# Attention and a 2-D Fourier filter on one core: stack rows loaded in pieces of 16 and 12, four butterflies and three transposes moved

## The chip, the cores and the metric

The kernel runs on one core of a Trainium2 chip, as one program. The metric is the device time of one execution in microseconds (us). The kernel before has a median of 712.09 us over three runs.

## The reference

Two results are computed and put side by side.

- Part A: attention with a compressive memory. `x` has 2048 rows of 576 numbers. `q`, `k` and `v` are `x` times three weight matrices, split into 32 heads of 18 numbers, and the rows into 4 segments of 512. In each segment and head: `softmax(q k^T / sqrt(18) + causal mask) v`, mixed by a gate for each head with `phi(q) M / (phi(q) z)`, where `M` and `z` are sums of `phi(k)^T v` and `phi(k)` over the earlier segments. The result goes through a last weight matrix `wo`.
- Part B: a real 2-D Fourier transform of a second 2048x576 array, a product with a complex filter, and the transform back.

Everything is float32; the kernel keeps that accuracy by splitting numbers into parts of fewer bits.

## The kernel before

Four stages follow each other, each written as Python generators that are advanced by hand, so the order of the instructions on each engine is the order in which the program emits them.

1. **Forward transform** (`FFT.forward`, about the first 65 us). The weights of `q` and `k` are loaded beside it.
2. **Projections** (`ATT.projections`, to about 277 us). For each segment `g` of 4 there are 9 units `qk_unit` (128 rows of `q` or `k` each) and 4 units `v_unit`. A `qk_unit` cuts its product into three bfloat16 planes `sp3`, and SyncE (SP) writes them to a DRAM tensor `qkD[g]` of 1152 x 3 x 512 (L498). A `v_unit` copies its product into a tile `vt` (two buffers; ScalarE, L521), and SP writes that to `vD` (L522). Between the units the butterflies and twiddles of part B run on VectorE (`bf`, L210). They are taken from one list by `Pace`: each unit takes a share `w` of the operations, worked out from `pace.left-8`, so that 8 of them remain for the next stage. In the last segment the last `v` units also split the first three `Y` tiles on VectorE (L285).
3. **Inverse transform** (`FFT.inverse`, to about 349 us). Step `u` of 16 does `i2` (matmuls, L300), an evacuation `T` on ScalarE and VectorE (L330 to L338), `i3` for step `u-2` (L311) and its output (L316 to L319); from `u=2` on each step takes one remaining butterfly. Beside it `ATT.prologue` does the first ten tiles of `s1` (below) and issues the first stack loads.
4. **Attention** (`ATT.attention`, to the end). A loop over 128 head tiles `t`, named as `t = 4k + hh`, with `k` for a group of 4 heads and `n = k // 2` for a **stack** of 8 heads. `s1(t+10)` computes scores to find the row maxima (L667, L675, L676 on TensorE, L671 and L677 on VectorE; three PSUM buffers `s1`). `mpath(k)` turns the maxima of four tiles into two rows of the stacked `Q`: split into two bfloat16 parts on GpSimd (L692, L693), transposed on TensorE (`mt`, L697), copied by ScalarE (L700) and written by a DMA that GpSimd issues (L701). `s2(t)` computes the scores again, shifted by the maxima, and their exponentials (L711 to L721); `pv` multiplies with `v` (L741). A list `bg` holds background work (memory part, output projection); its PSUM bank is `post`, one buffer.

What the change touches:

- **Stacks.** `Q` of a stack is a tile of 128 partitions x 8 heads x 512, of which 108 partitions are six pieces of 18 rows: the 18 numbers of a head, from one of the three planes. `K` has the planes in another order, so that the one matmul over 108 rows adds six products. `stack_dmas(n, qk)` makes the six DMAs, each 18 partitions x 8 heads x 1 KB (144 KB). They are issued by SP (L651). The first stack lies in a tile named `x`, the others in `Qs` and `Ks`; there are 3 tiles for `Q` and 4 for `K`.
- **SP's queue.** SP issues all its DMAs in the program's order. Each takes one of eight completion semaphores in turn, and waits until the last DMA that used this one has landed. In attention two entries of the list of loads are issued in each tile (`q.pop(0)`).
- **Maxima.** `mpath` takes the bank `post` for `mt` where `1<k<10`, and later one of the three `s1` buffers.

The lines on which the order hangs:

```
ap=bass.AP(tensor=a.tensor,offset=a.offset,ap=[[1536,18],[1536*18,8],[1,512]])
nc.sync.dma_start(T[18*pc:18*pc+18],ap)
...
p,a=(s.ps,"post") if 1<k<10 else (s.psm,s.mtag)
...
if hh==3 and m is not None: steps(m,1)
```

Of the kernel before, what the change touches and what calls it, by code (L numbers as in the profile page):

```python
# [102 lines left out]
class FFT:  # L103
# [183 lines left out]
    def inverse(s,yl,pp):  # L287

        nc,io=s.nc,s.io; tab,tab2=s.itab,s.itab2; v=nc.vector
        T={}; po={}; Yt=s.Yt  # L290
        def i2(u,cs):
            Y=Yt[u]; cc=s.civ[u]
            p=pp.tile([128,len(cs),256],F32,name="i2",tag="i3" if u==0 else "i2")
            for k,c in enumerate(cs):
                n=0
                for (i,hl) in ((0,0),(0,1),(1,0)):
                    for q in range(2):
                        o=128 if q==0 else 0
                        m=128 if c<2 else 99
                        nc.tensor.matmul(p[:m,k],Y[i][:,q,c*128:c*128+m],cc[:,hl,o:o+256],start=n==0,stop=n==5)  # L300
                        n+=1
            return p
        def i3(u):
            h,l=T.pop(u); po[u]=[]
            for r in range(2):
                p=pp.tile([128,FP],F32,name=f"i3{r}",tag="i3"); po[u].append(p)
                w=slice(r*128,(r+1)*128)
                L=[(h[:,0,w],tab[:,0,r,0]),(h[:,1,w],tab[:,0,r,1]),(h[:,0,w],tab[:,1,r,0]),(h[:,1,w],tab[:,1,r,1]),
                   (l[:,0,w],tab[:,0,r,0]),(l[:,1,w],tab[:,0,r,1]),(h[:99,2,w],tab2[:99,r])]
                for n,(x,t) in enumerate(L):  # L310
                    nc.tensor.matmul(p,x,t,start=n==0,stop=n==6)  # L311
                yield
        def out(u):
            b,a=divmod(u,4); p=po.pop(u)
            E=yl.tile([128,FP],F32,name="E")
            nc.scalar.copy(E,p[0])  # L316
            o=yl.tile([128,2,FP],F32,name="yout",bufs=3)
            v.tensor_tensor(o[:,0],E,p[1],op=OP.add)
            v.tensor_tensor(o[:,1],E,p[1],op=OP.subtract)  # L319
            pend.append(lambda: nc.sync.dma_start(io["yb"][4*a+b],o))  # L320
        pend=[]
        def flush():
            while pend: pend.pop(0)()
        for u in range(18):
            if u>15: flush()
            if u<16:
                h=yl.tile([128,3,256],F32R,name="T0",bufs=3); l=yl.tile([128,2,256],F32R,name="T1",bufs=3)
                T[u]=(h,l)
                p=i2(u,(0,1))
                nc.scalar.copy(h[:,:2],p)  # L330
                if 1<u<14: s.ysplit(u+2)
                v.tensor_tensor(l,p,h[:,:2].bitcast(F32),op=OP.subtract)  # L332
                yield
                flush()
                p=i2(u,(2,))
                Yt.pop(u); s.civ.pop(u)
                nc.scalar.copy(h[:99,2],p[:99,0])
                v.tensor_tensor(h[64:97,2],p[64:97,0],h[64:97,2].bitcast(F32),op=OP.subtract)  # L338
                if u==0: s.ysplit(3)
                if u+4<16: s.load_civ(u+4)  # L340
                yield
            if u>1:
                yield from i3(u-2)
                out(u-2)
                s.pace.take(1)
        flush()
BF=mybir.dt.bfloat16
H=32; DH=18; SC=float(DH)**-0.5
# [45 lines left out]
class ATT:  # L394
    def __init__(s,nc,tc,io,cp,dp):
        s.nc,s.tc,s.io=nc,tc,io
        s.ident=cp.tile([128,128],F32,name="ident"); s.bm=cp.tile([126,7,19],F32,name="bm")
        s.Mst=[None]+[cp.tile([126,5,126],F32,name=f"Mst{i}") for i in range(1,4)]
        s.zst=[None]+[cp.tile([126,5,32],F32,name=f"zst{i}") for i in range(1,4)]
        d=lambda n,sh,dt: dp.tile(sh,dt,name=n)  # L400
        s.qkD=[d(f"qkD{i}",[1152,3,512],BF) for i in range(4)]
        s.pqD=[None]+[d(f"pqD{i}",[576,512],F32) for i in range(1,4)]
        s.vD=[d(f"vD{i}",[4,128,622],F32) for i in range(4)]
        s.dp=dp
# [103 lines left out]
    def v_unit(s,g,tb,tp,pp):  # L508
        nc=s.nc
        P=[]  # L510
        for hf in range(2):
            ps=pp.tile([128,288],F32,name="pjv",tag="pj")
            yield from s.passes(ps,g,"wv",slice(288*hf,288*hf+288),slice(128*tb,128*tb+128),True)
            P.append(ps)
            yield
        vt=tp.tile([128,622],F32,name="vt")
        vv=vt[:,:608].rearrange("p (h c) -> p h c",c=19)
        nc.gpsimd.memset(vv[:,:,18:19],1.0)  # L518
        nc.gpsimd.memset(vt[:,608:],0.0)
        for hf in range(2):  # L520
            nc.scalar.copy(vv[:,16*hf:16*hf+16,:18],P[hf].rearrange("p (h c) -> p h c",c=18))  # L521
        nc.sync.dma_start(s.vD[g][tb],vt)  # L522
        if g==3: return
        for _ in range(3): yield
        if tb==0: s.pm=[pp.tile([126,3,7,19],F32,name=f"pm{i}",tag="pm") for i in range(2)]
        for t in range(5):
            w=7 if t<4 else 4; r=18*w
            nc.tensor.matmul(s.pm[t//3][:r,t%3,:w].rearrange("p h c -> p (h c)"),s.pk[:,tb,126*t:126*t+r],vt[:,133*t:133*t+19*w],  # L528
                start=tb==0 and t%3==0,stop=tb==3,skip_group_check=True)
        if tb<3: return  # L530
        yield
        n=g+1
        for t in range(5):
            w=7 if t<4 else 4; r=18*w
            m=tp.tile([126,7,19],F32,name="mm")
            nc.vector.tensor_tensor(m[:r,:w],s.pm[t//3][:r,t%3,:w],s.bm[:r,:w],op=OP.mult)
            z=s.zst[n][:r,t,:w]
            for o,h0,h1,c0,c1 in ((0,0,7,0,18),) if t<4 else ((0,0,2,0,18),(36,2,3,0,12),(48,1,2,6,18),(60,2,4,0,18)):
                k=(h1-h0)*(c1-c0)
                M,N=[x[:r,t,o:o+k].rearrange("p (h c) -> p h c",c=c1-c0) if x is not None else None for x in (s.Mst[n],s.Mst[g])]  # L540
                x=m[:r,h0:h1,c0:c1]
                if n==1: nc.gpsimd.tensor_copy(M,x)
                else: nc.gpsimd.tensor_tensor(M,x,N,op=OP.add)
            if n==1: nc.gpsimd.tensor_copy(z,m[:r,:w,18])
            else: nc.gpsimd.tensor_tensor(z,m[:r,:w,18],s.zst[g][:r,t,:w],op=OP.add)
    def projections(s,xp,tp,pp,wv,pace,hook):

        live=[]
# [2 lines left out]
        def advance():  # L551
            for l in list(live):
                try: next(l)
                except StopIteration: live.remove(l)
        tot=pace.left-8
        for g in range(4):
            if g<3: xq=[s.xprep(g+1,t,(xp,s.x0)[g%2],xp,[128,512],"xst",2) for t in range(5)]
            for i in range(13):
                u=s.qk_unit(g,i,tp,pp) if i<9 else s.v_unit(g,i-9,tp,pp)
                if i==4 and g<3: s.pk=tp.tile([128,4,576],F32,name="pk",bufs=1)  # L560
                next(u)
# [1 line left out]
                next(lw,None); next(lw,None)  # L563
                if g<3 and i in (4,6,8,10,12): next(xq[(i-4)//2])
                if g<3 and i in (1,3,5,7,9): next(xq[(i-1)//2])
                w=tot/(36-18*.3+12*2.7+4*2.0)*((2.7 if g<3 else 2.0) if i>8 else .7 if s.third(g,i) else 1.0)
                advance()
                pace.take(w*.7)
                advance()
# [72 lines left out]
    def stack_dmas(s,n,qk):  # L642

        nc=s.nc; g,G=divmod(n,4)
        L=[]
        T,base,order=((s.Qs[n%3],0,(0,0,0,1,1,2)),(s.Ks[n%4],576,(0,1,2,0,1,0)))[qk]
        for pc,o in enumerate(order):
            a=s.qkD[g][base+8*G*18:base+8*G*18+18,o]
            ap=bass.AP(tensor=a.tensor,offset=a.offset,ap=[[1536,18],[1536*18,8],[1,512]])
            def go(T=T,pc=pc,ap=ap):  # L650
                nc.sync.dma_start(T[18*pc:18*pc+18],ap)  # L651
                if pc==5: s.loaded.add((n,qk))
            L.append(go)
        return L
    def load_v(s,n):
# [29 lines left out]
    def mpath(s,k):  # L685
# [6 lines left out]
        nc.gpsimd.tensor_copy(mh[:,0],mg)  # L692
        nc.gpsimd.tensor_tensor(mh[:,1],mg,mh[:,0],op=OP.subtract)  # L693
        yield
        p,a=(s.ps,"post") if 1<k<10 else (s.psm,s.mtag)
        pt=p.tile([128,1024],BF,name="mt",tag=a)[:,:128]
        nc.tensor.transpose(pt,mh.rearrange("p a m -> p (a m)"),s.idb)  # L697
        yield
# [242 lines left out]
            if t<=now: f()  # L941
            else: s.late.append((t,f))
    def begin(s,sm,sp,ps1):
        s.late=[]; s.now=-1
        s.sm,s.sp,s.ps1=sm,sp,ps1
        s.mh=sm.tile([128,8,16],BF,name="mh",bufs=1); s.nc.gpsimd.memset(s.mh,0.0)
        s.mg={};s.mx={};s.m2={};s.P={};s.vs={};s.rc={};s.am={};s.amg={};s.pq={};s.ux={}
    def prologue(s):
# [7 lines left out]
        i=0  # L956
        for t in range(10):
            for _ in s.s1(t):
                for _ in range(1+(i%24==0)):
                    if q: q.pop(0)()  # L960
                i+=1
                yield
# [7 lines left out]
    def attention(s,tp,ps):  # L970
# [20 lines left out]
        for t in range(133):  # L991
# [24 lines left out]
            b=s.s2(t) if t<128 else iter(())  # L1016
            if q: q.pop(0)()
            if qu: qu.pop(0)()
            if hh==3 and m is not None: steps(m,1)
            steps(a,1)  # L1020
            steps(b,1)
            r=(t-5)%4
# [9 lines left out]
                qu+=[u[0],lambda: next(rb)]+u[1:]  # L1032
            steps(a,1)
            steps(b,1)
            if hh==2 and m is not None: steps(m,1)
            if hh==1 and k+2<32: m=s.mpath(k+2); next(m)
            if 7<=t<131 and t%4==3:
                s.pv_out((t-7)//4)
# [78 lines left out]
def emit(nc,tc,io):  # L1117
    def pool(es,name,bufs=1,**kw):
        return es.enter_context(tc.tile_pool(name=name,bufs=bufs,reuse_waits="tile",**kw))
    with ExitStack() as L0:  # L1120
# [9 lines left out]
        with tc.manual_schedule():  # L1130
# [5 lines left out]
            with ExitStack() as es:  # L1136
# [3 lines left out]
                def hook(g,i):  # L1140
# [5 lines left out]
                        F.inv_setup(ci)  # L1146
                    if g==3 and i>9: F.ysplit(i-10,nc.vector)
                    if g==3 and i==0: q0.extend(A.stacks0(x0))
                    for _ in range((0,2,2,2,2,1,1,1,1)[i] if g==3 and i<9 else 0): q0.pop(0)()
                q0=[]  # L1150
                A.projections(xp,tp,pp,wv,F.pace,hook)
            Rv.close()
# [36 lines left out]
```

## Time and profile before

| what | us |
|---|---|
| median of three runs (710.78 to 712.10) | 712.09 |
| the profiled execution, whole | 713.06 |
| its span, from the first to the last instruction | 711.3 |
| TensorE (PE) busy in the span | 673.6 |
| VectorE (DVE) busy | 558.6 |
| ScalarE (ACT) busy | 444.1 |
| GpSimd (POOL) busy | 216.7 |

PE is busy for 95% of the span, but the ends of its matmuls are modelled, so its busy time is not its work. Time is gained where PE waits, where its clock is lowered, or where it must wait for a buffer. The views used below are the page, the waits (who waited for whom, in total, with count and longest), the windows (busy time of PE, PEld, DVE, ACT and POOL with the number of instructions in each stretch, then the granted clock, the DMA engines' mean busy share and GB/s), the chain of work that ended last, and the timeline. SPq stands for SP's queue: a DMA issue. "DMA x<-qkD" is a stack piece that loads the tile `x`.

### The profile page before, as it was taken

How to read it: one execution, taken by the hardware profiler on the slowest of the kernel's cores; microseconds unless marked ns; L12 is line 12 of the kernel's file. 1: busy time of each engine (PE TensorE's matmuls, PEld its weight loads, DVE VectorE, ACT ScalarE, POOL GpSimd, SP SyncE). 2: the span in 40 equal slices, each digit the busy share in tenths (PEclk: the TensorE clock that was granted, in tenths of full speed). 3: DMA queues.
4: the chain of work that ended last, by engine and by line, in shares of the span. 5: the costliest groups of instructions: out<-in, count | busy, mean ns of one | idle time of the engine just before them, and what ended most of it. 6: DMA issues, size and time to landing. Idle time of an engine off the chain costs nothing.

```text
span 711.3 us, 14134 instructions
## 1 busy us (share of the span) xinstructions
PE 673.6 (95%) x4829; PEld 494.4 (70%) x4829; DVE 558.6 (79%) x1237; ACT 444.1 (62%) x999; POOL 216.7 (30%) x422
## 2 busy tenths in 40 slices
PE   5999999999999999999999799898999999998997
PEld 4999779889879788999744344443566445664676
DVE  6999999899989888897588588877656886568253
ACT  3657695584584563444487577776766677667741
POOL 2110000200200212575057443554324664246210
PEclk9999999999999999999999899999999999999999
DMA  9876546555564568889527666766656756442232
GB/s 344 274 230 202 150 144 194 170 185 164 166 209 137 174 219 262 201 242 245 164 74 191 172 154 147 175 164 149 150 135 173 177 152 147 125 135 68 91 98 80
DMA packets 83752, 121.56 MB, mean 171 GB/s; under 512 B 11498, under 2 KB 51032, under 8 KB 83544
## 3 DMA queue, kind: packets, MB, share of 16 engines
q1 hardware_dynamic: 77088, 104.62, 51.3%
q0 software_dynamic: 6592, 16.04, 8.1%
q8 instruction: 38, 0.62, 0.4%
q14 instruction: 34, 0.28, 0.1%
HBM read 82.30 MB, written 38.24 MB: 169 GB/s over the span
## 4 chain that ended last, share of the span: by engine, by line
PE 54%; DMA 12%; DVE 8%; ACT 6%; issue 3%; POOL 3%; SPq 1%; DVEq 0%; ACTq 0%; POOLq 0%
PE pv L741 7%; PE pj L468 6%; PE po L902 6%; PE pjv L468 6%; PE i L300 4%; PE i L311 4%; PE s L667 4%; DMA Ks<-qkD 4%; PE s L675 3%; DMA x<-qkD 3%; PE s L711 2%; DMA pq<-pqD 2%; PE po L934 2%; PE s L715 2%; PE pm L528 2%
## 5 line engine op out<-in xcount | busy, mean ns | idle before, releaser
L671 DVE CUSTOM_DVE_ANT_0 junk<-s,mask 128x512 bf16<-128x512 f32 (+1 forms) x256 | 141.5, 553 | 55.0 <-PE s L667 43.8
L677 DVE TENSOR_REDUCE mx<-s 128x4 f32<-128x512 f32 x128 | 87.8, 686 | 21.9 <-PE s L676 20.6
L712 ACT ACTIVATE P<-s 128x512 f32<-128x512 f32 x128 | 77.1, 602 | 26.5 <-PE s L711 25.1
L741 PE MATMUL pv<-P,vs 128*32 128x512 f32 (+3 forms) x1024 | 82.4, 440 | 0.0
L717 ACT ACTIVATE P<-s 128x512 f32<-128x512 f32 x128 | 76.8, 600 | 8.7 <-PE s L716 5.0
L721 ACT ACTIVATE P<-s 128x256 f32<-128x256 f32 x128 | 49.4, 386 | 46.7 <-PE s L720 46.7
L724 POOL TENSOR_SCALAR_AFFINE_SELECT P<-P 128x512 f32<-128x512 f32 x116 | 69.5, 638 | 5.1 <-ACT P L712 4.1
L741 PEld LDWEIGHTS pv<-P,vs 128*32 128x32 f32 x1024 | 26.8, 109 | 45.3 <-issue 41.9
L468 PE MATMUL pj<-x,wqkh 128*128 128x512 f32 x162 | 56.0, 406 | 0.0
L518 POOL MEMSET vt<- 128x32 f32 x16 | 2.4, 161 | 147.4 <-PE pm L528 120.4
L210 DVE TENSOR_TENSOR t<-Z 128x580 f32<-128x580 f32 x64 | 46.6, 755 | 0.1
L210 DVE TENSOR_TENSOR Z<-t 128x580 f32<-128x580 f32 x64 | 45.8, 753 | 0.0
L667 PE MATMUL s<-Ks,Qs 108*128 108x512 bf16 (+1 forms) x128 | 42.1, 329 | 0.0
L492 ACT CAST sp<-pj 128x512 bf16<-128x512 f32 x36 | 21.1, 586 | 30.6 <-DVE pj L488 30.6
L142 PE MATMUL f<-ftab,eh 128*128 128x290 f32 (+1 forms) x160 | 31.5, 316 | 8.7 <-DMA ftab<-ftab 8.6
L300 PE MATMUL i<-civ,Y 128*128 128x256 f32 (+1 forms) x288 | 37.9, 284 | 1.6 <-DVE T L332 1.6
L300 PEld LDWEIGHTS i<-civ,Y 128*128 128x128 f32 (+1 forms) x288 | 35.9, 181 | 1.8 <-DVE T L332 1.8
L468 PEld LDWEIGHTS pj<-x,wqkh 128*128 128x128 f32 x162 | 30.4, 188 | 8.4 <-issue 1.6
L311 PE MATMUL i<-itab,T 128*128 128x290 f32 (+1 forms) x224 | 36.1, 310 | 0.0
L468 PE MATMUL pj<-x,wqkl 128*128 128x512 f32 x90 | 35.6, 395 | 0.0
L468 PE MATMUL pj<-xh,wqkl 128*128 128x512 f32 x90 | 35.5, 395 | 0.0
L468 PE MATMUL pj<-xh,wqkh 128*128 128x512 f32 x90 | 35.5, 395 | 0.0
(227 smaller groups left out, 1834.5 us busy)
## 6 DMA issues: line engine op xcount, KB each, us to landing
qkD<-sp SPq DMA_DIRECT2D x36, 384.0 KB
Ks<-qkD SPq DMA_DIRECT2D x72, 144.0 KB
x<-qkD SPq DMA_DIRECT2D x60, 144.0 KB
Qs<-qkD SPq DMA_DIRECT2D x60, 144.0 KB
xin<-xb SPq DMA_DIRECT2D x16, 384.0 KB
cfw<-cfw POOLq DMA_DIRECT2D x16, 384.0 KB, 4.5
civ<-civ POOLq DMA_DIRECT2D x16, 384.0 KB, 7.1
vs<-vD SPq DMA_DIRECT2D x16, 330.0 KB
```

The lines of the kernel that those rows point to most:

```text
L210: v.tensor_tensor(o,a,b,op=op)
L300: nc.tensor.matmul(p[:m,k],Y[i][:,q,c*128:c*128+m],cc[:,hl,o:o+256],start=n==0,stop=n==5)
L311: nc.tensor.matmul(p,x,t,start=n==0,stop=n==6)
L468: s.nc.tensor.matmul(out,a,b,start=i==0,stop=i==len(L)-1)
L667: nc.tensor.matmul(out,Q[:108,h,128*i:128*i+128],K[:108,h,:128*(i+1)],start=True,stop=True)
L671: nc.vector.tensor_tensor_reduce(out=junk[:,:w],in0=src,in1=s.mask[:,512-w:],scale=1.0,scalar=-3.0e38, op0=OP.add,op1=OP.max,accum_out=s.m ...
L677: nc.vector.tensor_reduce(out=s.mx[k][:,hh],in_=pa.rearrange("p (b c) -> p b c",c=128),axis=mybir.AxisListType.X,op=OP.max)
L712: nc.scalar.activation(P[0][:,hh],p0,AF.Exp,scale=SC)
L717: nc.scalar.activation(P[1][:,hh],p1,AF.Exp,scale=SC)
L721: nc.scalar.activation(P[2][:,hh],p2,AF.Exp,scale=SC)
L724: if k<29: nc.gpsimd.affine_select(out=x,in_=x,pattern=pat+[[1,128]],compare_op=OP.is_ge,fill=0.0,base=0,channel_multiplier=-1)
L741: nc.tensor.matmul(s.pvt[32*hh:32*hh+32,128*j:],vt[:,j,19*h:19*h+32],mv[0][:,hh,mv[1]],start=j==0,stop=j==2,skip_group_check=True)
```

## The change

- `stack_dmas` makes seven DMAs in place of six: six of 16 partitions x 8 heads, with the first 16 rows of each piece, and one of 12 partitions x 8 heads with the two last rows of all six pieces. These come from a new DRAM tensor `reD`, which twelve DMAs for each segment (`rest`, 64 rows of 1 KB each, DRAM to DRAM, issued by SP) fill from `qkD`: six ahead of `v` unit 11, six ahead of unit 12. The matmuls still add over 108 rows, in another order.
- The last projection unit takes nearly none of the butterflies (weight 0.2 in place of 2.0), and 12 in place of 8 remain for the inverse transform, where steps from `u=6` on take two each.
- `mpath` also takes the bank `post` where the background list is empty and `t<116`. By the code's counts of steps this holds where `mt` would take an `s1` buffer in the tiles t=38, 42 and 46. For the last group (`k=31`) the transpose and the copy move from the end of t=118 and the start of t=119 to the start and the end of t=119.
- The prologue issues its longer list of stack loads with one extra in every 5 steps in place of every 24; the first stack's 14 pieces are issued two in each of six units, then one in two.

```diff
-                s.pace.take(1)
+                s.pace.take(1 if u<6 else 2)
...
+        s.reD=[d(f"reD{i}",[64,12,512],BF) for i in range(4)]
...
+    def rest(s,g):
+        L=[]
+        for qk in (0,1):
+            for pc,o in enumerate(((0,0,0,1,1,2),(0,1,2,0,1,0))[qk]):
+                a=s.qkD[g][576*qk+16:576*qk+17,o]; b=s.reD[g][32*qk:32*qk+32]
+                x=bass.AP(tensor=a.tensor,offset=a.offset,ap=[[1536*18,32],[1536,2],[1,512]])
+                y=bass.AP(tensor=b.tensor,offset=b.offset+512*2*pc,ap=[[512*12,32],[512,2],[1,512]])
+                L.append(lambda x=x,y=y: s.nc.sync.dma_start(y,x))
+        return L
...
-        tot=pace.left-8
+        tot=pace.left-12
...
+            rest=s.rest(g)
             for i in range(13):
+                for _ in range(6 if i>10 else 0): rest.pop(0)()
...
-                w=tot/(36-18*.3+12*2.7+4*2.0)*((2.7 if g<3 else 2.0) if i>8 else .7 if s.third(g,i) else 1.0)
+                w=tot/(36-18*.3+12*2.7+3*2.0+.2)*((2.7 if g<3 else 2.0 if i<12 else .2) if i>8 else .7 if s.third(g,i) else 1.0)
...
-        for pc,o in enumerate(order):
-            a=s.qkD[g][base+8*G*18:base+8*G*18+18,o]
-            ap=bass.AP(tensor=a.tensor,offset=a.offset,ap=[[1536,18],[1536*18,8],[1,512]])
+        for pc,o in enumerate(order+(0,)):
+            if pc<6:
+                a=s.qkD[g][base+8*G*18:base+8*G*18+18,o]
+                ap=bass.AP(tensor=a.tensor,offset=a.offset,ap=[[1536,16],[1536*18,8],[1,512]])
+            else:
+                a=s.reD[g][32*qk+8*G:32*qk+8*G+8]
+                ap=bass.AP(tensor=a.tensor,offset=a.offset,ap=[[512,12],[512*12,8],[1,512]])
...
-                nc.sync.dma_start(T[18*pc:18*pc+18],ap)
-                if pc==5: s.loaded.add((n,qk))
+                nc.sync.dma_start(T[16*pc:16*pc+(16 if pc<6 else 12)],ap)
+                if pc==6: s.loaded.add((n,qk))
...
-        p,a=(s.ps,"post") if 1<k<10 else (s.psm,s.mtag)
+        p,a=(s.ps,"post") if 1<k<10 or s.free else (s.psm,s.mtag)
...
-                for _ in range(1+(i%24==0)):
+                for _ in range(1+(i%5==0)):
...
-            if hh==3 and m is not None: steps(m,1)
+            if hh==(0 if k>29 else 3) and m is not None: steps(m,1)
...
-            if hh==2 and m is not None: steps(m,1)
+            s.free=not bg and t<116
+            if hh==(3 if k==29 else 2) and m is not None: steps(m,1)
...
-                    for _ in range((0,2,2,2,2,1,1,1,1)[i] if g==3 and i<9 else 0): q0.pop(0)()
+                    for _ in range((0,2,2,2,2,2,2,1,1)[i] if g==3 and i<9 else 0): q0.pop(0)()
```

More of the change, by code (lines that the diff above doesn't have):

```diff
@@ L943, in begin @@
     def begin(s,sm,sp,ps1):
-        s.late=[]; s.now=-1
+        s.late=[]; s.now=-1; s.free=False
         s.sm,s.sp,s.ps1=sm,sp,ps1
```

## The prediction

> **What bounds the kernel now.** I read the page's span and engine totals first, then who waited on PE, then the windows round the longest wait, the chain there, and SP's timeline under the chain.
>
> ```profile
> span 711.3 us, 14134 instructions
> PE 673.6 (95%) x4829; PEld 494.4 (70%) x4829; DVE 558.6 (79%) x1237; ACT 444.1 (62%) x999; POOL 216.7 (30%) x422
> ```
>
> PE is the engine that sets the pace; it idles 711.3 - 673.6 = 37.7 us in all. Only those gaps can be won, besides stretches in which PE is slowed. The waits of PE that have one cause:
>
> ```profile
> PE f L142 <- DMA ftab<-ftab: 8.6, 2, 7.7
> PE s L675 <- DMA Ks<-qkD: 4.6, 2, 3.6
> ...
> PE i L300 <- DVE T L332: 1.6, 1, 1.6
> ...
> PE mt L697 <- POOL mh L693: 1.4, 3, 0.7
> ```
>
> The first is the start of the program, which the change leaves alone. The second is a wait for stacks (4.6 us in two waits, 3.6 and 1.0), the third stands at the entry of the inverse transform, the last at the transposed maxima. So each part of the change has a wait of its own to aim at, and the stacks have the largest. What that wait costs is more than its idle time. The windows (busy time of PE, PEld, DVE, ACT, POOL; clock, DMA share, GB/s):
>
> ```profile
> 0.00:20.00 20.00, 11.29 (x60) 10.64 (x61) 13.31 (x28) 7.53 (x11) 4.63 (x14) 1.00 0.97 341
> 380.00:400.00 20.00, 15.63 (x133) 7.40 (x132) 13.25 (x42) 11.85 (x31) 13.01 (x18) 0.93 0.75 195
> 397.30:404.00 6.70, 5.28 (x25) 2.61 (x29) 3.21 (x8) 2.79 (x6) 1.64 (x4) 0.50 0.61 161
> 424.00:427.00 3.00, 3.00 (x31) 1.16 (x24) 1.79 (x7) 1.74 (x5) 0.42 (x2) 1.00 0.62 128
> 300.00:320.00 20.00, 19.96 (x159) 18.70 (x158) 17.99 (x44) 8.81 (x22) 13.22 (x21) 1.00 0.89 235
> ```
>
> PE is busy for only 15.63 of the 20 us from 380, and from 397.3 to 404 its granted clock is 0.50. The chain tells what PE waited for:
>
> ```profile
> 371.93 8.47 DMA x<-qkD
> 380.42 6.53 DMA x<-qkD
> 387.01 6.76 DMA pq<-pqD
> 393.79 4.91 DMA Ks<-qkD
> 398.72 0.59 PE s L675 x2
> ```
>
> From 371.93 to 398.70 the chain is DMA alone, and each issue in it stands where an earlier DMA landed (371.93 + 8.47 = 380.40, and the next starts at 380.42). SP's timeline shows why:
>
> ```profile
> 369.99 2.28 SPq L651 DMA_DIRECT2D x<-qkD  x6
> ...
> 380.42 0.27 SPq L651 DMA_DIRECT2D x<-qkD  x1
> ...
> 389.92 1.18 SPq L651 DMA_DIRECT2D Qs<-qkD  x2
> ```
>
> Between these rows SP issues 27 DMAs, 16 of them stack pieces (10 of `x`, 6 of `Qs`); the issue at 380.42 is the eighth after that of 371.93 and waits for its landing. With eight in flight the queue gets one landing per 8.47 / 8 = 1.06 us, although an issue itself takes 0.27. And the engines are not full while this goes on: from 424 to 427, with eight stack pieces under way and nothing else from SP, their mean share is 0.62 and they move 128 GB/s, against 0.97 and 341 GB/s in the first 20 us. A stack piece of 18 rows thus leaves over a third of the engines idle.
>
> **The stacks' pieces.** Before, a piece is 18 x 8 KB = 144 KB and takes 1.06 us of the queue. No row shows a piece of 16 or 12 rows, so I bound its price p (16 rows, 128 KB). From above: the same rate per byte, 1.06 x 128/144 = 0.94 us. From below: 131 KB at 341 GB/s, 0.38 us. I take 0.94 x 0.62/0.97 = 0.60 us, the first scaled by the shares, since the first 20 us show that these engines can be filled by the same queue. The piece of 12 rows then takes 0.75p. A stack goes from 6 x 1.06 = 6.4 us to 6.75 x 0.60 = 4.05.
>
> [...]
>
> The wait at 395 ended when the last of six `Qs` pieces landed. The 16 stack pieces ahead of it are 16/6 stacks: 17.0 us before, 18p = 10.8 after, so it lands 6.2 us earlier. The wait was 3.6 us, so it goes, with 2.6 us to spare; it stays in part if p is over (17.0 - 3.6)/18 = 0.74. The wait of 1.0 goes likewise. With it goes the half clock: in the window of 0.50, PE is waiting until 398.7 and works at half speed for the 5.3 us left, which costs 2.6 us. Together 3.6 + 1.0 + 2.6 = 7.2 us. Next in line behind the stack is PE itself, whose steady pace is read below.
>
> [...]
>
> What is added: 48 gathers and 2 x 16 more pieces on SP, each an issue of about 0.3 us:
>
> ```profile
> L651 SPq DMA_DIRECT2D Ks<-qkD x72: 265/281/522, 293.4 to 604.7; - x72
> ```
>
> In attention this is 2 more issues for each stack pair, 0.6 us of SP in over 15 us, hidden while SP waits for landings as it does now. The gathers stand in the projections ahead of the writes `vD` of the `v` units 1 and 2. For three segments I cost them at nothing: behind them wait `vD` writes, and a `vt` buffer is wanted only two units later. In the last segment that cover is thin:
>
> ```profile
> 270.38 6.57 DMA vD<-vt
> ...
> 277.06 0.06 ACT vt L521
> ...
> 281.09 0.70 DVE T L332
> 281.80 0.04 issue
> 281.84 1.22 PE i L300 x8
> ```
>
> ACT's copy of the last `vt` waits until 276.95 for this write to land; behind it on ACT stand the first two `T`, and PE waits for the second. Six gathers ahead of the write push its issue back by 6 x 0.3 = 1.8 us, and more if SP must wait for a semaphore turn; against that the landing should be shorter as the loads ahead drain. On the other side the four butterflies are gone:
>
> ```profile
> 276.55 2.77 DVE L210 TENSOR_TENSOR Z<-t 128x580 f32<-128x580 f32 x4
> ```
>
> At 2.77/4 = 0.69 us each, DVE reaches `T` 2.8 us earlier, but `T` cannot start before ACT's copy; of the gap of 1.6 us at most 0.9 is won. I take +0.5 us for this entry, between -0.9 (write not delayed) and +2.5 (write delayed by 1.8 and more).
>
> **The butterflies in the inverse transform.** Steps 6 to 9 lie in the window 300 to 320, where DVE is busy for 17.99 of 20 us and PE for 19.96. Four more of 0.69 make 20.8 us: DVE falls 0.8 us behind in all. Its buffers are doubled and the following steps have none, so I take +0.1 us, between 0 and the whole 2.8.
>
> **The transposed maxima.** The chain passes `pv` once in two tiles in the stretch without background work:
>
> ```profile
> 415.60 1.22 PE pv L741 x16
> 419.52 1.22 PE pv L741 x16
> ...
> 433.22 1.21 PE pv L741 x16
> 437.69 1.21 PE pv L741 x16
> 441.55 1.21 PE pv L741 x16
> ```
>
> A pair of tiles takes 441.55 - 437.69 = 3.86 us without `mt`, 3.92 with `mt` in `post` (415.60 to 419.52) and 4.47 with `mt` in an `s1` buffer (433.22 to 437.69). So each `mt` moved is worth 0.55 us, and three move: -1.65 us, between -1.65 and 0 (if VectorE's maxima set that pace). The last group's transpose waits 0.7 us for GpSimd in the row quoted; one background step now stands ahead of it, and I take -0.3 us, between -0.7 and +0.5, as its DMA now stands behind GpSimd's masks of that tile.
>
> **Sum.** -7.2 + 0.5 + 0.1 - 1.65 - 0.3 = -8.55 us. The profiled execution (713.06) would be 704.5, and the median of 712.09, which is 0.97 below it, 703.5.
>
> **The rivals.**
>
> 1. *The entry of the inverse transform turns bad.* The gathers hold `vD` back until `qkD` of the last unit has landed, PE waits 2.5 to 4 us more and its clock halves once more, 2.6 us. For it: SP takes everything in order, and ACT does wait for this write. Against it: the first six gathers read rows written long before. Result: -9.05 + 2.5 to 6.6, so 705.5 to 709.6.
> 2. *The pieces win, but less.* p lies near 0.8, the wait at 395 shrinks below the point at which the clock falls, and something else, such as the `pq` loads in the chain, is late next. Result: half of 7.2, so 707.1.
> 3. *A DMA costs the same whatever its rows.* With p = 1.06 for each of seven pieces a stack takes 7.4 us in place of 6.4. The wait at 395 grows by 16/6 = 2.7 us, that of 1.0 by the same, and another 1.7 us run at half clock: 2.7 + 2.7 + 1.7 - 1.95 + 0.6 = +5.75, so 717.8, slower. It decides if p is over 6.4/7 = 0.91. The rows do not say how the price goes with the rows; the share of 0.62 with a full queue speaks for engines left idle, and against it. [...]
> 4. *Nothing is won*: the stacks are late because SP was held before 369.99 by its other waits, and the rest is small. The chain of landings speaks against it. Result: 711 to 713.
>
> **How the numbers follow.** Forecast 0.62 (its own range 701.0 to 705.5), rival 1 0.15, rival 2 0.11, rival 3 0.06, rival 4 0.06. The range 700.5 to 709.5 holds the first three but for their edges. A measurement of this kernel can tell about 0.2%, 1.4 us, from no change. Faster by more: the first three, less a little for small gains, 0.86; same 0.06; slower 0.08.
>
> **What would show it.** Right: no wait of PE for `Ks<-qkD` or `Qs<-qkD` over 0.5 us; a clock of 1.00 from 300 on; SP's issues of stack pieces 0.3 us apart without waits for landings between; pairs of 3.92 at the three moved `mt`; the gap at the entry of the inverse under 2.5 us; no PE wait for DVE over 0.5 us in steps 6 to 9. Wrong: a stack wait that stays or moves to another tile, SP still waiting for landings at 1 us each, or a new stretch of half clock near 282.

## The result, and the profile after

The kernel after takes 720.12 us (median of 4 runs, 717.81 to 723.09), beside 712.10 us for the kernel before on the same chip (4 runs, 710.78 to 712.74). The ratio is 1.0117, with a 95% interval from 1.0074 to 1.0161: slower by about 8 us, where 8.6 us less was forecast. The profiled execution took 717.81 us, 4.75 more than that of before (713.06); it is the fastest of the four, so the trace below accounts for these 4.75 us, and what the other executions lost beyond them no view shows.

The page's span, and those waits of PE that answer to the ones shown of before:

```profile
span 716.1 us, 14217 instructions
...
PE f L142 <- DMA ftab<-ftab: 10.0, 2, 9.1
PE s L692 <- DMA pq<-pqD: 5.8, 1, 5.8
...
PE i L300 <- DVE T L332: 3.3, 1, 3.3
...
PE s L692 <- DMA x<-reD: 1.5, 1, 1.5
...
PE mt L714 <- POOL mh L710: 0.4, 1, 0.4
```

Both waits for stacks are longer, not gone (5.8 and 1.5 us, before 3.6 and 1.0, at tile 22 and tile 62 in both). The wait at the entry of the inverse transform is doubled (3.3, before 1.6). Only the last row became shorter (0.4, before 1.4). The windows of after (busy PE, PEld, DVE, ACT, POOL; clock, DMA share, GB/s):

```profile
284.36:291.19 6.83, 6.18 (x27) 6.18 (x28) 2.14 (x4) 2.13 (x6) 2.45 (x4) 0.50 0.71 204
300.00:320.00 20.00, 20.00 (x159) 18.87 (x158) 19.22 (x46) 9.22 (x23) 11.69 (x18) 1.00 1.23 222
...
403.83:410.65 6.82, 4.66 (x21) 2.38 (x25) 3.03 (x7) 2.28 (x6) 0.88 (x2) 0.50 0.79 163
```

There are now two stretches of half clock, one behind each long wait; the first is new. From 300 to 320 the DMA engines' share went from 0.89 to 1.23 (over 1, as the times of packets that overlap are added in full), and yet they moved 222 GB/s, not 235. So the engines are filled, as the change wanted, but not with more work: each packet takes longer (a 1 KB packet of SP's queue 101 ns in the mean, before 65).

Where PE starts at five landmarks shows where the time came from:

| PE starts (us) | before | after | behind by | step |
|---|---|---|---|---|
| first matmul after the wait for `ftab` | 9.38 | 10.78 | 1.40 | +1.40 |
| second block of `i` in the inverse transform | 281.84 | 285.01 | 3.17 | +1.77 |
| first tiles of attention's scores, after the next short wait | 351.67 | 357.34 | 5.67 | +2.50 |
| tile 22, after the wait for its stack | 398.72 | 405.99 | 7.27 | +1.60 |
| tile 62, before its wait | 493.84 | 498.00 | 4.16 | -3.11 |
| end of the span | 711.3 | 716.1 | 4.8 | +0.6 |

The first step is no part of the change: that wait was between 8.3 and 10.3 us in all the kernels of this study. The next three are the entry, its half clock and the stack. The gain comes between tile 22 and tile 62; about 1.6 us of it are the three transposes (3 x 0.53, worked out below), and the rest is not taken apart here.

**The entry.** SP's timeline of before, and then of after, between the last `qkD` write and the last `vD` writes:

```profile
270.38 7.76 SPq L522 DMA_DIRECT2D vD<-vt  x3
```

```profile
270.99 3.80 SPq L555 DMA_DIRECT2D reD<-qkD  x6
275.40 0.33 SPq L523 DMA_DIRECT2D vD<-vt  x1
277.20 3.88 SPq L555 DMA_DIRECT2D reD<-qkD  x6
281.19 0.99 SPq L523 DMA_DIRECT2D vD<-vt  x2
```

Before, three `vD` writes follow each other. After, six gathers hold SP for 3.80 us ahead of the second, six more for 3.88 us ahead of the third. The chain of after goes through these writes:

```profile
266.93 8.40 DMA vD<-vt
...
275.40 4.42 DMA vD<-vt
...
281.19 2.88 DMA vD<-vt
...
284.27 0.70 DVE T L332
...
285.01 4.21 PE i L300 x18
```

Two of these starts are waits for landings. The second write is the eighth DMA behind the first (a `qkD` write and six gathers stand between), so it has the same semaphore and starts where the first has landed (266.93 + 8.40 = 275.33). The second six gathers read rows of the last unit's `qkD` and waited for that write, as SP's waits from 268 to 285 show:

```profile
SPq L555 <- DMA qkD<-sp: 1.5, 1, 1.5
SPq L523 <- DMA vD<-vt: 0.5, 1, 0.5
```

VectorE's second `T` starts as soon as the third write has landed (281.19 + 2.88 = 284.07). It reads nothing of that write, so it must take over the memory of its `vt` (no view shows addresses); PE waits for `T`.

**The stack for tile 22.** The chain of after there:

```profile
391.47 8.38 DMA Qs<-qkD
399.87 6.07 DMA pq<-pqD
405.99 0.58 PE s L692 x2
```

As before, an issue stands where an earlier DMA landed: 391.47 + 8.38 = 399.85, and the next is at 399.87. With eight under way that is one landing per 8.38 / 8 = 1.05 us, where it was 1.06. The eight are not alike, though: six pieces and two `pq` loads here, four pieces and four other transfers in the row of before. The same list of loads is better compared as a whole. SP's first piece behind an `ob` load went out at 369.99 before, and at 375.65 after:

```profile
375.65 1.84 SPq L668 DMA_DIRECT2D x<-qkD  x4
```

From there to PE's start at tile 22 it took 398.72 - 369.99 = 28.73 us before and 405.99 - 375.65 = 30.34 after, 1.6 us more. PE came to the tile 0.6 us sooner in this count, which makes the 2.2 us by which the wait grew.

### The profile page after: what moved, and what is told of

Its sections match the earlier page's. It is cut to its first block, busy times and chain, and to the rows that moved or that the text cites. A ratio compares the mean times of both kernels' runs of the same rounds, so it can differ in the third digit from the quotient of the medians.

```text
span 716.1 us, 14217 instructions
## 1 busy us (share of the span) xinstructions
PE 674.7 (94%) x4829; PEld 496.4 (69%) x4829; DVE 558.0 (78%) x1237; ACT 443.5 (62%) x999; POOL 215.1 (30%) x422
## 4 chain that ended last, share of the span: by engine, by line
PE 65%; DVE 11%; DMA 10%; ACT 8%; issue 4%; POOL 1%; SPq 0%; ACTq 0%; DVEq 0%; POOLq 0%
PE pv L758 9%; PE pj L469 7%; PE po L919 6%; PE pjv L469 5%; PE s L684 5%; PE i L300 4%; PE i L311 4%; PE s L692 4%; PE s L728 3%; PE s L732 2%; DMA vD<-vt 2%; PE po L951 2%; DMA Qs<-qkD 2%; PE pm L529 2%; DMA xin<-xb 2%
## 5 line engine op out<-in xcount | busy, mean ns | idle before, releaser
L300 PE MATMUL i<-civ,Y 128*128 128x256 f32 (+1 forms) x288 | 39.7, 293 | 3.3 <-DVE T L332 3.3
L300 PEld LDWEIGHTS i<-civ,Y 128*128 128x128 f32 (+1 forms) x288 | 37.5, 189 | 3.5 <-DVE T L332 3.5
```

## The experiments

Twelve kernels were run. Each ratio is to the kernel before on the same chip. "Tile 22" and "entry" are the waits of PE in the profiled execution, "half clock" the stretches of clock 0.50 between the start and the end.

| run | edit | median us | ratio, 95% | tile 22 | entry | half clock, us |
|---|---|---|---|---|---|---|
| before | | 712.10 | | 3.6 | 1.6 | 6.8 |
| after | | 720.12 | 1.0117 (1.0074 to 1.0161) | 5.8 | 3.3 | 6.8 + 6.8 |
| e1 | before + butterflies + maxima | 714.13 | 1.0027 (0.9998 to 1.0056) | 4.5 | 0.8 | 3.4 + 3.4 |
| e2 | before + pieces and gathers | 718.08 | 1.0077 (1.0047 to 1.0107) | 6.4 | 4.0 | 6.8 + 6.8 + 3.4 |
| e3 | after, last gathers late | 713.17 | 1.0010 (0.9991 to 1.0028) | 6.7 | 0.8 | 10.2 |
| e4 | after, rows on every sixth partition | 712.25 | 0.9994 (0.9978 to 1.0011) | 2.8 | 3.6 | 3.4 + 6.8 |
| e5 | after, reads joined | 715.44 | 1.0038 (1.0011 to 1.0066) | 4.0 | 3.3 | 3.4 + 6.8 |
| e6 | e3 + e4 | 708.61 | 0.9934 (0.9911 to 0.9957) | 2.4 | 1.3 | 3.4 |
| e7 | after, `pq` loads 8 tiles later | 714.78 | 1.0022 (0.9991 to 1.0053) | 1.3 | 3.1 | 3.4 + 6.8 |
| e8 | before, rows on every sixth partition | 708.06 | 0.9922 (0.9892 to 0.9951) | 2.2 | 1.6 | 3.4 |
| e10 | e6 + e7 | 705.31 | 0.9879 (0.9842 to 0.9915) | none | 0.8 | none |
| e11 | e8 + butterflies + maxima | 704.63 | 0.9877 (0.9829 to 0.9926) | 0.8 | 0.9 | none |
| e12 | e11 + `pq` loads later | 703.48 | 0.9848 (0.9812 to 0.9883) | none | 0.8 | none |
| e13 | after, rows on every second partition | 713.72 | 1.0008 (0.9983 to 1.0033) | 4.1 | 3.6 | 3.4 + 6.8 |

The theory to be tried (A): the partitions that a piece writes set its price, and 16 neighbours are dear. (That they share few ways into SBUF was the author's supposition; no view shows such ways or counts them.) Against it stand B (the reads of 1 KB rows, 3 KB apart, are the limit) and C (the number of transfers in SP's turn is, whatever they carry). For the entry: the gathers ahead of `vD`, against the butterflies or the loads.

### e1 and e2: the parts alone

e1 is the kernel before with all of the diff but `rest`, `reD`, the new pieces and the prologue's two changes of pace; e2 has only these:

```diff
 # e2, against the kernel after
-                s.pace.take(1 if u<6 else 2)
+                s.pace.take(1)
...
-        p,a=(s.ps,"post") if 1<k<10 or s.free else (s.psm,s.mtag)
+        p,a=(s.ps,"post") if 1<k<10 else (s.psm,s.mtag)
```

> The kernel before with the butterflies and the transposed maxima changed and the stacks left in pieces of 18 rows. Theory (the stacks and their gathers are the whole loss): the three moved maxima give 3 x 0.55 = 1.65 us, the last group's transpose 0.1 to 0.3, the butterflies 0 to 0.9 at the entry of the inverse transform, where the wait of PE for T was 1.6 us in the kernel before. So 712.1 - 1.75 to 2.85 = 709.3 to 710.4 us, no half clock near 282, the stack wait of about 3.6 us still there at tile 22. Rival (the butterflies cost PE in steps 6 to 9, or the maxima only look cheaper): 712 us or more.

> The kernel after with the butterflies and the maxima put back, so that the new pieces and the gathers stand alone. Theory (the stacks and their gathers are the whole loss, the rest is a gain of about 2 us): 720.1 + 1.75 to 2.85 = 722 to 723 us, with the stack wait near 5.8 us at tile 22 and the long wait at the entry of the inverse both there. Rival (moving the butterflies is what makes the entry bad): the wait of PE for T near 282 falls back to about 1.6 us without half clock, and the time to 717 us or less.

The stack part alone is slower than before, and the entry is as bad with the butterflies in their old place. The waits of PE in e2:

```profile
PE s L692 <- DMA rD<-U: 6.4, 1, 6.4
...
PE i L300 <- DVE T L332: 4.0, 1, 4.0
```

So the loss is the stacks' and the gathers', and the entry is not the butterflies' doing. But both times missed: e2's median is 4 us under its forecast (the profiled execution, 722.13, was in it), and e1 gained nothing. e1's waits of PE, and a window behind one of them:

```profile
PE s L675 <- DMA Ks<-qkD: 6.4, 2, 4.5
...
PE i L300 <- DVE T L332: 0.8, 1, 0.8
...
PE mt L697 <- POOL mh L693: 0.4, 1, 0.4
```

```profile
470.80:474.20 3.40, 3.40 (x11) 1.34 (x10) 1.60 (x4) 1.97 (x5) 0.00 (x0) 0.50 0.59 172
```

The entry (1.6 to 0.8) and the transpose (1.4 to 0.4) did gain. PE reached tile 22 at 394.06, 1.1 us sooner than before, and went on at 398.55, nearly as before (398.72): the stack's landing sets that point, so the wait took the gain. A second wait for a stack came up at 468 (6.4 - 4.5 = 1.9 us), with 3.4 us of half clock behind it. Here a saving of PE ahead of a load that comes late was no saving; e11 tries this.

### e3: the last segment's gathers out of the way

```diff
-                for _ in range(6 if i>10 else 0): rest.pop(0)()
+                for _ in range(6 if i>10 and g<3 else 0): rest.pop(0)()
...
+            if t==0: q+=s.rest(3)
             if hh==0 and qd==0:
```

> The kernel after, with the last segment's 12 gathers issued in the attention's first tile instead of ahead of its third and fourth v unit. Theory (the gathers ahead of vD make the wait of 3.3 us and the half clock of 6.83 us at the entry): the wait falls back to 0.7 to 1.6 us, the clock stays at 1.00 there, 1.7 to 2.6 us and 3.1 us are won, so 720.1 - 4.8 to 5.7 = 714.4 to 715.3 us; the wait at tile 22 stays at 5 to 7 us. Rival (the wait at the entry comes from the loads ahead of vD, which share the engines with it, not from the gathers): 719 us or more, with the gap still over 2.5 us.

```profile
PE s L692 <- DMA pq<-pqD: 6.7, 1, 6.7
...
PE i L300 <- DVE T L332: 0.8, 1, 0.8
```

The wait at the entry fell to 0.8 us, its half clock went, and the time fell by about 7 us (ratio 1.0117 to 1.0010), somewhat more than the 4.8 to 5.7 forecast. The gathers made the bad entry. The wait at tile 22 stayed, as both theories had it.

### e4, e5, e13 and e8: what makes a piece slow

```diff
 # e4
-                nc.sync.dma_start(T[16*pc:16*pc+(16 if pc<6 else 12)],ap)
+                nc.sync.dma_start(T[pc:pc+91:6] if pc<6 else T[96:108],ap)
 # e13
+                o=32*(pc//2)+pc%2; nc.sync.dma_start(T[o:o+31:2] if pc<6 else T[96:108],ap)
 # e8, on the kernel before
-                nc.sync.dma_start(T[18*pc:18*pc+18],ap)
+                nc.sync.dma_start(T[pc:pc+103:6],ap)
 # e5
-                ap=bass.AP(tensor=a.tensor,offset=a.offset,ap=[[1536,16],[1536*18,8],[1,512]])
+                ap=bass.AP(tensor=a.tensor,offset=a.offset+pc*512*128 if pc<3 else a.offset+(pc-3)*512*128,ap=[[512*8,16],[512,8],[1,512]])
```

(In e5, `a` also starts at plane 0 for all pieces. Its stacks hold other rows than attention needs, so e5 serves for its times alone.)

> The kernel after, with the rows of a 16-row piece written to every sixth partition of the stack instead of 16 neighbours (the piece of 12 rows to the last 12 partitions as before). The order of the rows in the stack is changed by that, so the products of the queries and keys are those of other rows; the bytes, the number of transfers and their engines are the same. Theory A (a piece is limited by the few ways into SBUF that 16 neighbouring partitions share): the price of a piece falls from about 0.8 to 0.5 to 0.6 us, the wait of 5.8 us at tile 22 goes, with its half clock (about 2 to 3 us) and the wait of 1.5 us at tile 62, DMA share over 300 to 320 falls under 1, so 720.1 - 8 to 10 = 710 to 712 us, with the entry of the inverse as bad as it was. Theory B (the reading of 1 KB packets from DRAM limits it) and theory C (SP's semaphore turn with the landings of other transfers limits it): 719 to 721 us, the wait at tile 22 still 5 us or more.

> The kernel after, with each 16-row piece read from one stretch of 128 KB that lies together in DRAM, where the change reads rows of 1 KB that lie 3 KB apart. So the stacks hold other rows of the projections than they should; what is written to SBUF, its partitions, the bytes, the number of transfers and their engines are the same. Theory A (the neighbouring partitions limit a piece): as the kernel after, 718 to 721 us, tile 22 still waits 5 us or more, DMA share over 300 to 320 stays above 1.1. Theory B (the reading of spread packets limits it): the share falls under 1 and the wait at tile 22 to 3 us or less, 711 to 715 us. Both may hold in part; then it lies between.

> The kernel after, with a piece of 16 rows written to every second partition of a block of 32 (two pieces to a block), the piece of 12 rows as before; queries and keys are dealt alike, so the products are the same. A dose between neighbours and every sixth. By the theory of the few ways into SBUF, twice as many are reached as by neighbours: the packets of 1 KB take between the 107 ns of neighbours and the 46 ns of every sixth in the stretch 300 to 320, the DMA share there lies between 0.87 and 1.23, and the time between 712 and 720 us. Rival (what helped was the longer issue, which keeps SP from overfilling the queue, whatever the partitions): packets and share as with every sixth, since the partitions are not neighbours here either and the issue takes as long, 712 us.

> The kernel before, with its pieces of 18 rows written to every sixth partition of the stack instead of 18 neighbours: no new pieces, no gathers, no other edit; the queries and the keys are dealt alike, so the products are the same. Theory A (a piece is limited by the ways into SBUF that neighbouring partitions share): with 9 engines a piece is not held by them much, as each packet took 59 to 65 ns where the pieces of 16 rows took 95 to 107, so at most 0.1 to 0.2 us of 1.06 are won for each and the wait of 3.6 us at tile 22 falls to 0.5 to 3 us: 709 to 712 us. Rival (the engines that a piece runs on are all that counts before): no change, 712.4 us, the wait still 3 to 4 us.

One sentence of e4's expectation is mistaken: queries and keys are dealt alike, so the matmul adds the same products in another order. And the "twice as many" ways of e13's is part of the author's supposition: the runs show prices, not ways.

A DMA view of the window from 300 to 320 gives for SP's queue the packets, the MB and the share of the 16 engines' time. In turn: before, after, e5, e13, e4, e8.

```profile
q1 hardware_dynamic: 2416, 2.98, 53.8%
```

```profile
q1 hardware_dynamic: 2521, 2.96, 74.9%
```

```profile
q1 hardware_dynamic: 1174, 2.96, 74.1%
```

```profile
q1 hardware_dynamic: 2667, 3.26, 61.7%
```

```profile
q1 hardware_dynamic: 2718, 3.14, 53.2%
```

```profile
q1 hardware_dynamic: 2490, 3.11, 46.3%
```

Sixteen engines over 20 us are 320 us of engine time, so the price of a MB is the share x 320 / MB. Before: 0.538 x 320 / 2.98 = 57.8 us. After: 81.0. With joined reads, and less than half the packets: 80.1. With the rows on every second partition: 60.6; on every sixth: 54.2; and the old pieces of 18 rows on every sixth: 47.6. The pieces' bytes and reads are the same in after, e4 and e13; their partitions differ, and the length of an issue (below). That is what theory A says, with a dose between.

These prices mix the pieces with the `yb` writes, which SP's queue carries in the same window in packets of 2320 bytes. Taken apart by packet size in the traces, the `yb` packets cost 42 to 46 us for a MB in all six kernels, and the pieces 63.9 before, 98.8 after, 71.5 in e13, 58.9 in e4 and 50.1 in e8. So on SP's queue only the pieces became dearer. In e5 they cost 90.1: the reads (B) are about a tenth of the price, and not what made it rise, since the kernel before reads the same rows of 1 KB.

From neighbours to every second partition the price of a piece of 16 rows falls by 28% (98.8 to 71.5 us for a MB), and from there to every sixth by another 18% (to 58.9). The pieces of before do not fit into this row by their partitions alone: they also write neighbours, and their 63.9 lies under the 71.5. They have fewer packets under way at once. By the packet records, each packet counted at 40 ns (their commonest distance is 42), a piece of 18 rows that overlapped no other piece had at most 9 of 1 KB under way in before (three pieces, from 254.2, 257.5 and 260.0 us), and a piece of 16 rows had 16 in after (from 258.9 us). That agrees with the 9 engines of e8's expectation, though the records name no engine. That 9 at a time hold each other up less than 16 would explain the 63.9, but no run tries this. That the partitions set the price is shown; by what means they do is not.

Times follow. e4 is level with the kernel before, although its entry is as bad as in after (3.6 us). The wait at tile 22 fell to 2.8 us, not to nothing as forecast. e8, one line in the kernel before, gains 0.8%, more than forecast. Its waits and e4's:

```profile
PE s L675 <- DMA Ks<-qkD: 2.2, 1, 2.2
```

```profile
PE i L300 <- DVE T L332: 3.6, 1, 3.6
PE s L692 <- DMA Ks<-qkD: 2.8, 1, 2.8
```

Spreading also makes an issue longer. SP's issues of the `Qs` pieces (min, median, max in ns) in after, and then in e4:

```profile
L668 SPq DMA_DIRECT2D Qs<-qkD x60: 302/429/498, 293.5 to 597.6; - x60
```

```profile
L668 SPq DMA_DIRECT2D Qs<-qkD x60: 554/598/1288, 292.3 to 593.1; - x60
```

That longer issue is not what helped, at least not all: in e13 it is the same (median 598) with a higher price and a wait of 4.1 us. Nor does it set the pace where the stack for tile 22 is loaded. The chains of e13 and then of e4 there:

```profile
391.88 7.04 DMA Qs<-qkD
398.94 5.84 DMA pq<-pqD
```

```profile
392.89 6.50 DMA Qs<-qkD
399.40 2.37 DMA Ks<-qkD
```

As in after, the second issue waits for the landing of the first, eight turns back: a landing per 0.88 us in e13 and 0.81 in e4, beside 1.05 in after. The eight transfers are of the same kinds in e13 as in after; in e4 a small `rD` write stands in place of one piece. In e5 the wait at tile 22 fell to 4.0 us and the half clock at the entry to 3.4, and the time to 715.4, between the theories: so the joined reads save something too.

### e6, e7 and e10: the change mended

```diff
 # e7
-            if 16<=t<21: s.pq_load(1,t-16)
+            if 24<=t<29: s.pq_load(1,t-24)
```

> Both changes that helped alone: the pieces spread to every sixth partition, and the last segment's gathers in the attention's first tile. If they add up: the entry saves 2.9 us of wait and a half clock of 3.4 us, the landing of the stack for tile 22 comes 4.2 us sooner than with the gathers alone moved (400.5 in that run), so the wait falls from 6.7 to about 2.5 us: 713.2 - 4.2 - 1 to 2 for the clock = 707 to 708 us, faster than the kernel before by 0.6%. If the 12 gathers cost as much on SP in the attention as they did ahead of vD (12 x 0.6 = 7 us of issue): the wait at tile 22 stays at 4 us or more and the time at 710 to 712 us.

> The kernel after, with the five pq loads of the attention's tiles 16 to 20 moved to tiles 24 to 28; nothing else. They stand on SP between the Qs pieces that tile 22 waits for; in the kernel after the wait ended at 405.94 with the landing of a pq load in the chain. Theory C (the number of transfers in turn on SP's queue sets the wait, so five fewer ahead of it help by their share): five transfers at about 0.8 us each are 4 us, so the wait at tile 22 falls from 5.8 to 1 to 2.5 us, its half clock shortens or goes, and the time is 720.1 - 4 to 7 = 713 to 716 us. Theory A alone (the pieces themselves are too slow, whatever else is in the queue): the wait stays over 4 us and the time at 718 us or more.

> The kernel after with three edits: the pieces of 16 rows spread to every sixth partition, the last segment's gathers in the attention's first tile, the pq loads of tiles 16 to 20 moved to tiles 24 to 28. Against the run with the first two alone (708.6, a wait of 2.4 us at tile 22 and half clock for 3.4 us): if the queue now has room, the wait goes with its half clock, 708.6 - 2.4 - 1.7 = 704.5 us. Rival (the five loads only move the wait to the next stack, as they did without the spreading, where 2.7 us came up near 417): 707 to 709 us.

e6 adds e3 and e4: 708.61 us, 0.6 over its forecast, with a wait of 2.4 us for the 2.5 forecast. In e7, five transfers fewer ahead of the stack cut the wait at tile 22 from 5.8 to 1.3 us. That agrees with C, but does not show it: four of the five carry 252 KB and one 144 KB, as much as nine pieces, so their bytes may count as well as their number. And the queue had no room to take them later, and the second of its two waits for `Ks` came up near 417:

```profile
PE s L692 <- DMA Ks<-qkD: 4.0, 2, 2.7
```

In e10 with the spread rows a wait of 1.7 us came up there too, without half clock, and the time is 705.31 us.

### e11 and e12: the best of it without the new pieces

```diff
 # e11: e1 and e8 together; e12: with e7's line
```

> The kernel before with its pieces of 18 rows spread to every sixth partition, and the butterflies and the maxima of the change; no new pieces and no gathers. Theory (the gain of butterflies and maxima is real, and was eaten in the run without the new pieces by waits for stacks that came late): now the maxima's 1.65 us and the 0.2 us of the last group show, and of the 0.8 us at the entry most goes into the wait at tile 22: 708.1 - 1.9 to 2.7 = 705.4 to 706.2 us. Rival (the two parts are worth nothing by themselves): 708 us. Against the same parts with pieces of 16 rows and gathers (708.6): if engines per piece still count once the partitions are spread, this one is the slower; if not, the faster, by the gathers that it saves.

> As the run just above (pieces of 18 rows spread, butterflies, maxima), and the pq loads of tiles 16 to 20 moved to tiles 24 to 28. If the wait at tile 22 is the last one for a stack and the queue has room behind it: 2 to 2.5 us of wait and 1.7 us of half clock go, so 705.8 - 3.7 to 4.2 = 701.6 to 702.1 us. Rival (the wait moves to a later stack): 704 to 706 us.

In e11 the butterflies and maxima, which gained nothing in e1, come with 0.45% less (ratio 0.9922 to 0.9877; the medians differ by 3.4 us, and the intervals overlap). Part of that is the wait at tile 22, which fell from 2.2 to 0.8 us and lost its half clock, although PE had less to do ahead of it; why the stack came sooner is left open. And pieces of 18 rows are not slower than those of 16: e11 has 0.9877 where e6 has 0.9934, and e12 has 0.9848 where e10 has 0.9879 (on one chip, every run of e12 under every run of e10). Once the partitions are spread, the seventh transfer, the gathers and the prologue's other pace together cost more than the pieces of 16 rows bring. In e12 no wait for a stack is left, and PE idles only in short pieces from 380 to 400:

```profile
380.00:400.00 20.00, 19.59 (x174) 9.66 (x173) 17.06 (x53) 15.65 (x39) 15.38 (x24) 1.00 0.57 172
```

At 703.48 us (701.99 to 703.80, 4 runs; 1.5% under before) it beats both kernels. It is 1.4 us over the upper end of its forecast; the `pq` loads gave 1.2 us by the medians, with overlapping runs.

## Why the prediction was wrong, point by point

- **The price of a piece failed.** The step was "I take 0.94 x 0.62/0.97 = 0.60 us, the first scaled by the shares, since the first 20 us show that these engines can be filled by the same queue". The share did rise, but as packets that take longer: 81.0 in place of 57.8 us of engine time for a MB. The row that the estimate leaned on was no piece: SP's loads in those 20 us are mostly `xin`, 384 KB over 128 partitions, and all of its queue there (3.76 MB, 55.0% of the engines) cost 0.550 x 320 / 3.76 = 46.8 us for a MB. In the prediction's own sum the loads for tile 22, which took 1.6 us more in place of 6.2 less, make p = (17.0 + 1.6) / 18 = 1.03 us, where 0.60 was forecast and 0.74 was the break-even. The 1.06 too was no piece's price alone, as only four of the eight turns behind it were pieces.
- **So the 7.2 us were not won.** The wait at tile 22 grew by 2.2 us. That is the outcome of rival 3 (price 1.06 for each of seven pieces, growth 2.7 us), which had a chance of 0.06; its reason, a DMA that costs the same whatever its rows, was not the one: e4 and e13 change the price with rows and bytes as they were. The 1.7 us of half clock in its sum was the author's estimate, which no row of before shows; behind the second wait for a stack, 1.5 us at tile 62, the clock of after stayed at 1.00, and a stretch that cost about as much is in e1 (3.40 us of clock 0.50, PE busy in all of it: 1.7 us by estimate). The outcome came together with rival 1, a sum that the prediction gave no price and no chance.
- **The entry failed.** The step was "I take +0.5 us for this entry". Rival 1 came instead: 1.7 us more of wait and 6.83 us of half clock, in which PE was busy for 6.18 and so lost 3.1 by estimate (the chain's 18 matmuls of `i` took 4.21 us there, and 2.40 in before). Its argument against, that the first six gathers read rows written long before, was true and did not help: these six held the second write by their number, and the second six did wait 1.5 us for `qkD` of the last unit, as the rival said. The issue was mis-sized: "each an issue of about 0.3 us" was read from loads into SBUF, and a gather from DRAM to DRAM took 0.59:

```profile
L555 SPq DMA_DIRECT2D reD<-qkD x48: 528/595/2109, 115.4 to 280.5; - x48
```

- **The third write was not followed.** Without the butterflies VectorE was done at 278.0 us. It waited 3.2 us for ScalarE's first `T`, and after its own first `T` another 2.0 us for the third `vD` write. The prediction had only the second write, through ScalarE.
- **The butterflies in steps 6 to 9 were right**: PE lost nothing there, against +0.1 us, as it is busy for 20.00 of 20 us from 300 in after.
- **The maxima were right**: a pair of tiles with `mt` now takes 444.09 - 440.15 = 3.94 us (forecast 3.92), without it 3.86. The chain's `pv` rows of after:

```profile
440.15 1.21 PE pv L758 x16
...
444.09 1.21 PE pv L758 x16
...
447.95 1.22 PE pv L758 x16
```

The last group's transpose won as well: its wait of 0.7 us for GpSimd is gone, and all such waits fell from 1.4 to 0.4 us. But what such steps are worth by the clock depends on the stacks: nothing in e1, up to 3.4 us with the entry in e11.

## What to carry to other kernels

A share of the DMA engines below one is no room by itself: here it rose from 0.89 to 1.23, and the engines moved 222 GB/s in place of 235. Ask which partitions the pieces write (98.8 us for a MB on 16 neighbours, 58.9 on every sixth), and price a new transfer by a row with the same partitions, not by the fullest row of the profile. Count the engine time for each MB before and after (57.8 and 81.0 here); if it rises with the share, the packets take longer (65 to 101 ns here) and the share is no more work. And where loads come late, work taken off TensorE ahead of them may only lengthen the wait, as in e1 (3.6 to 4.5 us at tile 22), so mend the loads first and judge the small steps after that.

## What the runs showed of the hardware that was not expected

- The same pieces cost 98.8 us of engine time for a MB on 16 neighbouring partitions, 71.5 on every second and 58.9 on every sixth (81.0, 60.6 and 54.2 with the `yb` writes of the same queue). GpSimd's queue, which loads `civ` meanwhile, paid too: 46.6% of the engines for 1.44 MB in after, 32.4% for 1.61 in e4.
- An SP issue of a `Qs` piece with every sixth partition took 0.60 us in the median for 16 rows (0.43 with neighbours), and 0.75 for 18 rows (0.34).
- The clock fell also behind waits shorter than the 3.6 us of before: 3.4 us of half clock followed the wait of 1.9 us in e1, and those of 2.2 us in e8 and 2.4 in e6. The wait of 1.7 us in e10 was followed by none. If the length of a wait alone set it, rival 2's point at which the clock falls would lie between 1.7 and 1.9 us; whether it does is not settled here.
